# Halved blocks, output buffers and the last product of an attention-plus-gated-product kernel

## The chip, the core and the metric

The kernel runs on one NeuronCore of a Trainium2 chip. The metric is the device time of one execution in microseconds. Seven names recur: PE is TensorE's matmuls and PEld its weight loads, DVE is VectorE, ACT is ScalarE, POOL is GpSimd, SP is SyncE, and PSUM banks are where matmuls leave their sums (512 float32 columns on 128 partitions each).

## What is computed

The reference, cut to its core. There are 8 batches, 12 heads, 448 tokens of 64 numbers per head; the second part works on 3584 tokens of 768 numbers with 2048 hidden ones.

```python
scores = scale * np.matmul(q, k.transpose(0, 1, 3, 2))
attn = softmax(scores)                      # over the keys
x = np.matmul(attn, v)                      # heads side by side: (3584, 768)
h = x @ w_in                                # (3584, 2048)
g = h * (1.0 / (1.0 + np.exp(-h)))          # the gate
out = g @ w_out                             # (3584, 768), float32
```

## The kernel before

**Order.** Nothing is written in program order by hand. A planner (class `Order`, L111, with the loop at L1880) holds a queue of operations with durations and due times, and decides which engine does what next; the instructions are then emitted in that order (L1937). Each engine executes its own instructions strictly in sequence, with semaphores between the engines. A change of a few conditions in the planner can therefore move instructions far away from the edit.

**Attention.** A unit is a batch and a group of four heads (24 units, L987). For each unit, TensorE multiplies keys and queries in tiles of 32 rows (`score`, L436), ACT takes the exponential (`expo`, L479), TensorE forms sums and products with the values in strips of 32 columns (`attend_alone`, `attend_own`, `attend_shared`), and DVE transposes, inverts and scales (`inverse`, L611, and `norm`, L642) into the tile `xT`, which has the tokens in its columns. Batch 0's third group of heads is done in two halves of 224 tokens (`PIECES`, L253; the extra units 24 and 25), so that work on the first half can begin early.

**First product.** `ffn1` (L684) multiplies 128 hidden columns of `w_in` (a block; there are 16) with the tokens of a batch: six matmuls, one for each 128 rows of `w_in`. In batch 0 it does this for each half of the tokens by itself (224 columns), and puts two blocks side by side into one bank, so that one tanh on ACT and one gate on DVE (`tanh` L702, `gate` L734) cover 448 columns. Later batches use all 448 tokens and one block per bank. `queue_ffn1` (L1147) queues this; `blocks(b)` (L699) says how many blocks share a bank. Four banks, taken in turn, serve the attention sums, the first products and the outputs until the scores are finished. While attention is in progress, full-width products may be issued as four strips of 32 columns (`times`, L670).

**Batches 4 to 7** use a form of Strassen's seven products for the first matrix product (`pair_product`, L833), with operands combined by DVE into buffers that attention has finished with (`HOME`, L825; tags `E0` to `E9` are the exponentials' buffers).

**Second product.** Batch 0's first tiles are multiplied plainly (`plain`, L926). All other output tiles go in pairs, "quads" 1 to 13, again by seven products m = 1 to 7 of 8 steps each (`product`, L910; 384 columns a step). Products 1, 6, 7 and 4 add up in one bank, 5 and 3 in a second, 2 in a third. What a bank holds is read between: ACT copies it to a buffer `ost` (`take_copy`, L976), DVE adds a bank to that buffer (`take_sum`, L981). The order of products is 1, 5, 6, 2, 7, 3, 4. `store` (L956) then writes a finished buffer of 128 rows to memory in pieces of 32, 64 or 128 rows, from SP or in turn from SP and ACT. There are four `ost` buffers; quads 11 and 13 (`FAR`) use `xT` buffers instead.

**The end.** The last instructions are product 4 of quad 13 (8 matmuls of 384 columns), ACT's copy of its bank, and two stores of 64 rows, one from SP and one from ACT.

Of the kernel before, what the change touches and what calls it, by code (L numbers as in the profile page):

```python
# [9 lines left out]
FP16 = mybir.dt.float16  # L10
# [204 lines left out]
def kernel(  # L215
# [25 lines left out]
    OH = DM // 2  # L241
    NRK, NRQ = 2, 4
    PACE = 2.6
    NPL = 4
    EAGER = 1
    HALVES = 0
# [2 lines left out]
    SHY = 0.5  # L249
    AWAIT = 1.0  # L250
    FAR = (NT * B // 4 - 3, NT * B // 4 - 1)
    TWB, SXB = 40, 4
    PIECES = ((0, 7), (7, TPP))  # L253
    BURSTS = (
# [427 lines left out]
    h_t, th_t, o_t = {}, {}, {}  # L682

    def ffn1(b, f, t0, t1, strips, c0, c1):  # L684
        i = f % blocks(b)
        if i == 0 and c0 == 0:
            h_t[(b, f, t0)] = psum_bank(f"h_{b}_{f}_{t0}")
        h = h_t[(b, f - i, t0)]
        for cc in range(c0, c1):
            times(  # L690
                h[:, (t1 - t0) * i : (t1 - t0) * (i + 1)],
                w_in_t[:, cc, 128 * f : 128 * (f + 1)],
                x3(b, cc)[:, cc % 3, t0:t1],
                cc == 0,
                cc == NDC - 1,
                strips,
            )

    def blocks(b):  # L699
        return 2 if b == 0 else 1  # L700

    def tanh(b, f, t0, t1):  # L702
        n = (t1 - t0) * blocks(b)
        th = sb.tile([128, n], FP16, name=f"th_{b}_{f}_{t0}", tag="th", bufs=3)
        nc.scalar.activation(out=th, in_=h_t[(b, f, t0)][:, 0:n], func=AF.Tanh)  # L705
        th_t[(b, f, t0)] = th
# [27 lines left out]
    def gate(b, f, t0, t1):  # L734
        r = b % 2
        cut = 6 * 128 - S if b == 1 else S
        for lo, hi, dst, at in ((0, cut, G, S * r), (cut, S, X, -cut)):
            lo, hi = max(lo, t0), min(hi, t1)
            if b == 0 and lo < hi:
                nc.vector.scalar_tensor_tensor(  # L740
                    out=G[:, f : f + 2, t0:t1],
                    in0=th_t[(b, f, t0)].rearrange("p (f t) -> p f t", f=2),
                    scalar=1.0,
                    in1=h_t[(b, f, t0)][:, 0 : 2 * (t1 - t0)].rearrange("p (f t) -> p f t", f=2),
                    op0=ALU.add,
                    op1=ALU.mult,
                )
            elif lo < hi:
                nc.vector.scalar_tensor_tensor(  # L749
                    out=dst[:, f, at + lo : at + hi],  # L750
                    in0=th_t[(b, f, t0)][:, lo - t0 : hi - t0],
                    scalar=1.0,
                    in1=h_t[(b, f, t0)][:, lo - t0 : hi - t0],
                    op0=ALU.add,
                    op1=ALU.mult,
                )
# [150 lines left out]

    BANK = {1: 1, 6: 1, 7: 1, 4: 1, 2: 2, 5: 5, 3: 5}

    def product(qd, m, f0, f1, strips):  # L910
        w = {1: rows(2 * qd, 0), 2: rows(2 * qd, 1), 4: rows(2 * qd + 1, 1), 7: rows(2 * qd + 1, 0)}
        w = w[m] if m in w else S_t[(qd, m)]
        if BANK[m] == m and f0 == 0:
            pr_t[(qd, m)] = psum_bank(f"p_{qd}_{m}")
        for f in range(f0, f1):
            times(
                pr_t[(qd, BANK[m])][:, 0:OH],
                w[:, f, :],
                W_[m][:, f, :],
                f == 0 and BANK[m] == m,  # L920
                f == HF - 1,
                strips,
            )
# [19 lines left out]
    def bank(qd, m):  # L943
        return pr_t[(qd, m)][:, 0:OH]

    def ost(qd, i, j):
        name = f"ost_{qd}_{i}{j}"
        if qd in FAR:
            t = sb.tile([128, 3, S], FP16, name=name, tag="xT", bufs=NX3)
            t = t.rearrange("p c t -> p (c t)")[:, 0 : 2 * OH].bitcast(FP32)  # L950
        else:
            t = sb.tile([128, OH], FP32, name=name, tag="ost", bufs=NOST)
        ost_t[(qd, i, j)] = t
        return t

    def store(qd, i, j):  # L956
        u, t = divmod(2 * qd + i, NT)
        w, turn = 0, 0
        while w < 4:
            r, col = divmod(128 * t + 32 * w, S)  # L960
            b = 2 * u + r
            dst = out[b * S : (b + 1) * S, OH * j : OH * (j + 1)]
            if b == B - 1:
                n = 4 if w == 0 and qd < LAST else 2
                dst = dst[col : col + 32 * n]
            else:
                n = 1
                dst = dst.rearrange("(i g) m -> g i m", g=TPP)[col // 32]
            eng = nc.scalar if turn % 2 and 4 * qd + 8 >= NT * B else nc.sync
            eng.dma_start(out=dst, in_=ost_t[(qd, i, j)][32 * w : 32 * (w + n), :])  # L970
            w, turn = w + n, turn + 1

# [3 lines left out]
    def take_copy(qd, m):  # L976
        nc.scalar.copy(out=ost(qd, *OUT[m]), in_=bank(qd, BANK[m]))  # L977
        if m == 4:
            store(qd, *OUT[m])

    def take_sum(qd, m):  # L981
        t = ost_t[(qd, *SUM[m])]
# [137 lines left out]
    x_left = {}  # L1120
    ffn1_left = {b: 0 for b in range(B)}
    sg_ring, ost_ring = Ring(NSG), Ring(NOST)
    far_ring = Ring(NX3)
    STORE = 3.0
    pr_op, sg_op, w_op, plain_op = {}, {}, {1: [], 2: [], 3: []}, {}
    inv_op = []
# [11 lines left out]
    def gates_at(t, f):  # L1138
        if t % NT == NT - 1 and t // NT in KEPT:
            return [keep_op.get((t // NT, f // HF))]  # L1140
        made = []
        for b in {(128 * t + c) // S for c in (0, 127)}:
            x = g_op.get((b, f), [])
            made += x if len(x) >= (len(PIECES) if b == 0 else 1) else [None]
        return made

    def queue_ffn1(b, g0, g1):  # L1147
        t0, t1, parts = 32 * g0, 32 * g1, []
        begun = {}
        for f in range(NFF) if b == 0 else [x for f in range(HF if b < PB else FILL) for x in (f, f + HF)]:  # L1150

          half = 6 if b else NDC
          for c0 in range(0, NDC, half):

            def run(f=f, c0=c0):
# [2 lines left out]
                op = Op("PE", half * mm(t1 - t0), lambda: ffn1(b, f, t0, t1, strips, c0, c1), tail=PE_OUT)  # L1158
                if warm["on"]:
                    warm["on"] = False  # L1160
                n = blocks(b)
                if f % n == 0 and c0 == 0:
                    take_bank(f"h_{b}_{f}_{t0}")
                od.on_pe(op, "cols" if strips else "full", half * (4 if strips else 1))
# [24 lines left out]
            def deps(f=f, c0=c0):  # L1189
                if c0:  # L1190
                    return [] if begun.get(f) == c0 else [None]
                if f % blocks(b) and f - 1 not in parts:
                    return [None]
                made = [(x_op[(b, cc, g0)], cc * mm(t1 - t0)) for cc in range(NDC)] + ld_win[f]

                u, r = divmod(b, 2)
                for qd in range(NT * B // 4) if u else ():
                    if any(t // NT == u - 1 and (r or t % NT < 4) for t in (2 * qd, 2 * qd + 1)):
                        made += (
                            [plain_op.get(x) for x in ((0, 0), (0, 1), (1, 0), (1, 1))]  # L1200
                            if qd == 0
                            else [pr_op.get((qd, m)) for m in (1, 2, 3, 4, 7)]
                        )
                return made

            moe.append((deps, int(f % blocks(b) == 0 and c0 == 0), run, ()))
          ffn1_left[b] += 1

    pair_w, pair_x = {}, {}
# [80 lines left out]
    def queue_pair_f(pb, f):  # L1290
# [22 lines left out]
        def queue(m):  # L1313
# [6 lines left out]
            def run():  # L1320
# [7 lines left out]
                done[m] = op  # L1328
                if pb == PAIRS[0] and f == (3 if FILL < 4 else HF - 1) and m == 4:
                    last_pair.append(op)  # L1330
                if m == 1:
                    read("p", "ACT", lambda: pair_copy(pb, f, "p", "A"), [op], None, -3)
                elif m == 5:
# [59 lines left out]
    def queue_plain(t, j):  # L1393
# [6 lines left out]
        def queue(f0, f1):  # L1400
# [17 lines left out]
            def deps():  # L1418
# [2 lines left out]
                made = [ld_wout[i] for i in range(len(ld_wout)) if wout_rows[i] < f1]  # L1421
                for f in range(f0, f1):
                    x = g_op.get((0, f), ())
                    if len(x) < len(PIECES):
                        return [None]
                    made += x
                return made
# [56 lines left out]
    def queue_quad(qd):  # L1484
        quads.append((qd, [5, 6, 7, 3]))
        took = {}
        home = far_ring if qd in FAR else ost_ring

        def read(m, deps):
            def then(at):  # L1490
# [7 lines left out]
            bias = -2 if eng == "ACT" else -4  # L1498
            took[m] = od.add(Op(eng, busy, lambda: fn(qd, m), deps, bias, then=then))

        def queue(m, f0, f1):
            first = {6: (1,), 2: (1,), 7: (6, 5), 3: (5, 6) if qd == LAST else (5, 6, 7), 4: (7,)}.get(m, ())

            def run():
                strips = od.mode == "cols" and bool(qk_seq or av_seq)
                op = Op(
                    "PE", (f1 - f0) * mm(OH), lambda: product(qd, m, f0, f1, strips), tail=PE_OUT
                )
                if BANK[m] == m and f0 == 0:
                    take_bank(f"p_{qd}_{m}")  # L1510
                for ring, need in rings:
                    ring.take(need)
                if m in (5, 6, 3) and f1 == HF:
                    op.then = lambda at: sum_read(qd, m, at)
                od.on_pe(op, "cols" if strips else "full", (f1 - f0) * (4 if strips else 1))
                if f1 < HF:
                    begun[m] = f1
                    return
                pr_op[(qd, m)] = op
                read(m, [op] + [took[x] for x in {2: (1,), 7: (5,), 3: (6,)}.get(m, ())])  # L1520

            def deps():
                if f0:
                    return [] if begun.get(m) == f0 else [None]
                made = list(w_op.get(m, [None]))
                hard = {6: (1,), 7: (6,), 3: (5,), 4: (7,)}.get(m, ())
                made += [took.get(x) if x in hard else (took.get(x), 9.0) for x in first]
# [11 lines left out]


        begun = {}
        for m in (1, 5, 6, 2, 7, 3, 4):
            for f0 in range(0, HF, 1):
                queue(m, f0, f0 + 1)

    def after_x(n):

# [4 lines left out]
        else:  # L1552
            after_piece(b, g0, g1)

    def after_piece(b, g0, g1):
        x_left[(b, g0)] = x_left.get((b, g0), NG) - 1
        if x_left[(b, g0)]:
# [3 lines left out]
        if b >= PB:  # L1561
            return
        queue_ffn1(b, g0, g1)
        if g1 < TPP:
            return
        if b == 0:
# [402 lines left out]
```

## Time and profile before

| | us |
|---|---|
| median of 3 runs | 381.12 (380.66 to 381.26) |
| the profiled execution | 380.37 |
| its span, first to last instruction | 378.6 |
| TensorE busy in the span | 372.4 |
| DVE, ACT, POOL busy | 269.7, 255.5, 84.9 |
| granted TensorE clock | 1.0 |

The profile shows one execution. A group of instructions is given with its line, engine, operation and tile, how many there were, their busy time and the mean duration of one, which for pipelined matmuls is longer than the distance from one to the next. What an engine waited for is named by its releaser. The chain follows the end of the execution back, at each step to what released it, and can be listed in order of time. The order of a program's instructions on each engine is known without a run and holds no times.

### The profile page before, as it was taken

To read this page: it belongs to the slowest core of one execution; us is meant where nothing else is said; L and a number is where in the kernel's file an instruction comes from. 1 tells how busy PE (TensorE), PEld (TensorE's weight loads), DVE (VectorE), ACT (ScalarE), POOL (GpSimd) and SP (SyncE) were. 2 spreads that over 40 slices of the span, in tenths; PEclk is the share of its full clock that TensorE was granted. 3 is DMA by queue.
4 is the path that set the end of the run, shared out by engine and by line. 5 is a ranking of instruction groups with operands and counts; after the bars stand their busy time and mean duration, and the time that the engine had idled before them with its cause. 6 is when DMAs were issued, how large, how long until landed. Compare 5 with 4: busy or idle time off the path is not lost.

```text
span 378.6 us, 9949 instructions
## 1 busy us (share of the span) xinstructions
PE 372.4 (98%) x4024; PEld 191.5 (51%) x4024; DVE 269.7 (71%) x553; ACT 255.5 (67%) x400; POOL 84.9 (22%) x155
## 2 busy tenths in 40 slices
PE   7999999999999999999999999999999999999995
PEld 3367664444444444444444454545555555556663
DVE  3666859899995869995969998898475424446541
ACT  4988874897768787877788777658872238882221
POOL 6652438451007326006423200000000000000000
PEclk9999999999999999999999999999999999999999
DMA  7999999946139948148955421200002331002343
GB/s 120 191 208 210 206 204 186 190 53 98 17 92 124 184 49 124 26 94 116 170 86 73 54 53 34 68 18 0 3 1 59 94 74 26 0 2 59 84 110 83
DMA packets 35854, 34.47 MB, mean 91 GB/s; under 512 B 11872, under 2 KB 35040, under 8 KB 35808
## 3 DMA queue, kind: packets, MB, share of 16 engines
q0 software_dynamic: 25312, 22.82, 40.3%
q1 hardware_dynamic: 10080, 10.53, 10.6%
q8 instruction: 31, 0.51, 0.5%
q10 hardware_dynamic: 416, 0.49, 0.4%
q14 instruction: 15, 0.12, 0.1%
HBM read 45.61 MB, written 11.01 MB: 150 GB/s over the span
## 4 chain that ended last, share of the span: by engine, by line
PE 97%; DMA 1%; ACT 1%; DVE 0%; issue 0%; POOLq 0%
PE p L673 32%; PE h L673 21%; PE f L673 16%; PE s L438 12%; PE a L558 8%; PE o L673 3%; PE a L544 2%; PE a L591 2%; DMA rk<-in_k_dram 1%; ACT T L483 1%; PE z L1872 0%; PE z L673 0%; PE z L544 0%; DVE KT L387 0%; ACT ost L977 0%
## 5 line engine op out<-in xcount | busy, mean ns | idle before, releaser
L494 ACT ACTIVATE E<-s 128x896 f16<-128x896 f32 x164 | 142.0, 923 | 23.7 <-PE s L438 23.6
L673 PEld LDWEIGHTS <-w_in_t 128*128 128x128 f16 (+1 forms) x981 | 61.3, 97 | 45.2 <-issue 8.4
L673 PE MATMUL h<-xT,w_in_t 128*32 128x448 f16 (+2 forms) x834 | 84.0, 333 | 0.0
L344 POOL DMA_DIRECT2D V<-in_v_dram x88 | 48.4, 557 | 52.5 <-PE a L558 32.2
L673 PEld LDWEIGHTS <-G 128*128 128x128 f16 (+1 forms) x637 | 43.4, 97 | 32.4 <-issue 5.2
L977 ACT COPY ost<-p 128x384 f32<-128x384 f32 x52 | 24.9, 479 | 50.4 <-PE p L673 31.9
L705 ACT ACTIVATE th<-h 128x448 f16<-128x448 f32 x67 | 36.6, 546 | 22.8 <-PE h L673 19.1
L673 PE MATMUL p<-w_out_t,G 128*128 128x384 f16 (+1 forms) x343 | 51.9, 326 | 0.0
L438 PE MATMUL s<-rq,KT 32*128 32x448 f16 (+3 forms) x728 | 45.4, 347 | 1.3 <-DVE rq L402 1.0
L983 DVE TENSOR_TENSOR ost<-p,ost 128x384 f32<-128x384 f32 x39 | 21.6, 553 | 31.3 <-PE p L673 14.3
L673 PEld LDWEIGHTS <-S 128*128 128x128 f16 (+1 forms) x330 | 29.5, 98 | 23.5 <-issue 4.2
L673 PE MATMUL p<-D,S 128*128 128x384 f16 (+1 forms) x214 | 37.5, 326 | 0.0
L558 PE MATMUL a<-E,V 128*32 128x448 f16 (+1 forms) x640 | 32.9, 356 | 0.0
L749 DVE SCALAR_TENSOR_TENSOR G<-th,h 128x448 f16<-128x448 f16 (+1 forms) x52 | 28.8, 565 | 4.5 <-ACT th L705 3.9
L324 POOL DMA_DIRECT2D rq<-in_q_dram x25 | 13.8, 553 | 67.3 <-PE s L438 57.7
L661 DVE SCALAR_TENSOR_TENSOR xT<-a,rdn 128x448 f16<-128x448 f32 x46 | 27.0, 618 | 2.7 <-PE a L558 2.0
L438 PEld LDWEIGHTS <-KT 32*128 32x128 f16 (+1 forms) x824 | 12.5, 96 | 30.3 <-issue 28.1
L507 DVE TENSOR_TENSOR T<-T,E 128x1792 f16<-128x1792 f16 x20 | 21.7, 1086 | 3.9 <-ACT E L494 3.8
L876 DVE TENSOR_TENSOR p<-f,p 128x448 f32<-128x448 f32 x15 | 9.4, 624 | 20.4 <-PE f L673 13.5
L673 PE MATMUL f<-sx,tw 128*128 128x448 f16 x102 | 23.5, 352 | 0.0
L507 DVE TENSOR_TENSOR T<-E,E 128x1792 f16<-128x1792 f16 x20 | 21.6, 1082 | 2.5 <-ACT E L494 2.5
L558 PEld LDWEIGHTS <-V 128*32 128x32 f16 (+1 forms) x640 | 13.7, 95 | 18.0 <-issue 10.3
(95 smaller groups left out, 430.2 us busy)
## 6 DMA issues: line engine op xcount, KB each, us to landing
out_dram<-ost SPq DMA_DIRECT2D x194, 48.0 KB, 1.6
rk<-in_k_dram POOLq DMA_DIRECT2D x24, 224.0 KB, 5.0
rq<-in_q_dram POOLq DMA_DIRECT2D x23, 224.0 KB, 5.6
w_out_t<-in_moe_w_out_dram POOLq DMA_DIRECT2D x4, 768.0 KB, 12.5
V<-in_v_dram POOLq DMA_DIRECT2D x42, 64.0 KB, 4.1
V<-in_v_dram POOLq DMA_DIRECT2D x42, 48.0 KB, 4.3
w_in_t<-in_moe_w_in_dram POOLq DMA_DIRECT2D x6, 256.0 KB, 9.0
w_in_t<-in_moe_w_in_dram POOLq DMA_DIRECT2D x3, 512.0 KB, 12.3
```

The source lines that it names most:

```text
L324: nc.gpsimd.dma_start(out=rawq[n][:, cols], in_=group_of(q, b, hg)[:, cols])
L344: nc.gpsimd.dma_start(out=VT[b][32 * x : 32 * (x + 1), hs, at : at + count, :], in_=v[b, hs].rearrange("h (i g) d -> i h g d", g=TPP)[:, : ...
L438: nc.tensor.matmul(out=pS[p0 : p0 + 32 * (x1 - x0), h % 2, at : at + q1 - q0], lhsT=KT[(b, hg)][32 * h : 32 * (h + 1), key_rows(b, hg, c, ...
L494: nc.scalar.activation(out=E[(n, w)][:, 2 * y : 2 * y + 2, :], in_=pS_t[(n, w, y)][:, :, 0:S], func=AF.Exp, scale=attn_scale,)
L507: nc.vector.tensor_tensor(out=T[n], in0=T[n] if step else E[(n, 0)], in1=E[(n, step + 1)], op=ALU.add,)
L558: nc.tensor.matmul(out=a[32 * h : 32 * (h + 1), 0:S], lhsT=VT[b][k0:k1, HG * hg + h, place(b, hg, c), part - 1 :: 2], rhs=e[k0:k1, h], sta ...
L661: nc.vector.scalar_tensor_tensor(out=x3(b, cc)[:, cc % 3, 32 * g0 : 32 * g1], in0=acc[(n, part)][:, 0:nq], scalar=0.5, in1=rdn_t[n].rearra ...
L673: nc.tensor.matmul(out=out[i : i + cut], lhsT=w[:, i : i + cut], rhs=x, start=start, stop=stop, skip_group_check=True,)
L705: nc.scalar.activation(out=th, in_=h_t[(b, f, t0)][:, 0:n], func=AF.Tanh)
L749: nc.vector.scalar_tensor_tensor(out=dst[:, f, at + lo : at + hi], in0=th_t[(b, f, t0)][:, lo - t0 : hi - t0], scalar=1.0, in1=h_t[(b, f, ...
L977: nc.scalar.copy(out=ost(qd, *OUT[m]), in_=bank(qd, BANK[m]))
L983: nc.vector.tensor_tensor(out=t, in0=bank(qd, BANK[m]), in1=t, op=ALU.add)
```

## The change

Four things change, and the planner is told of each.

1. In batch 0 only blocks 0 to 3 are done in halves of the tokens (`BF0 = 4`). Blocks 4 to 15 wait for both halves, use 448 columns and one bank each, and have one tanh and one gate each. 
2. The outputs of quad 8 (`WIDE`) go to two of the ten `E` buffers, two outputs to each, in place of the four `ost` buffers. Those two held the first combined operands of batches 4 and 5, and count as free when the last block of that pair is done.
3. In the last quad product 2 comes last, and in two halves of 192 columns, each in a bank of its own. DVE adds each half to the buffer when it is done (`take_end`), SP stores the first half's 128 rows, SP and ACT store 64 rows each of the second.
4. The last quad's product 4, no longer last, is stored as one piece of 128 rows from ACT.

```diff
+    BF0 = 4
+    WIDE = NT * B // 4 - 6
...
-    def blocks(b):
-        return 2 if b == 0 else 1
+    def blocks(b, f):
+        return 2 if b == 0 and f < BF0 else 1
...
-    def product(qd, m, f0, f1, strips):
+    half_t = {}
+
+    def product(qd, m, f0, f1, strips, c0=0, c1=OH):
...
         if BANK[m] == m and f0 == 0:
-            pr_t[(qd, m)] = psum_bank(f"p_{qd}_{m}")
+            pr_t[(qd, m)] = psum_bank(f"p_{qd}_{m}" + "r" * (c0 > 0))
+        if c1 - c0 < OH:
+            half_t[c0] = pr_t[(qd, m)]
         for f in range(f0, f1):
             times(
-                pr_t[(qd, BANK[m])][:, 0:OH],
+                pr_t[(qd, BANK[m])][:, 0 : c1 - c0],
                 w[:, f, :],
-                W_[m][:, f, :],
+                W_[m][:, f, c0:c1],
...
+        elif qd == WIDE:
+            at, x = int(i != j), j
+            if at not in wide_t:
+                wide_t[at] = sb.tile(
+                    [128, HG, S], FP16, name=f"wide_{at}",
+                    tag=f"E{e_slot[f'sx_{PAIRS[0]}_{at + 1}']}", bufs=1,
+                )
+            t = wide_t[at].rearrange("p h s -> p (h s)").bitcast(FP32)
+            t = t[:, S * x : S * x + OH]
...
-                n = 4 if w == 0 and qd < LAST else 2
+                n = 4 if w == 0 and (qd < LAST or (i, j) == OUT[4]) else 2
...
+            if qd == LAST and (i, j) == OUT[4]:
+                eng = nc.scalar
...
+    def take_end(p, c0, c1):
+        t = ost_t[(LAST, 0, 0)][:, c0:c1]
+        nc.vector.tensor_tensor(out=t, in0=p, in1=t, op=ALU.add)
+        row = out.shape[0] - 256
+        for lo, eng in ((0, nc.sync), (64, nc.scalar)) if c0 else ((0, nc.sync),):
+            hi = lo + 64 if c0 else 128
+            eng.dma_start(out=out[row + lo : row + hi, c0:c1], in_=t[lo:hi])
...
-        for f in range(NFF) if b == 0 else [x for f in range(HF if b < PB else FILL) for x in (f, f + HF)]:
+        for f in range(BF0 * (g1 - g0 == TPP), NFF if g1 - g0 == TPP else BF0) if b == 0 else [x for f in range(HF if b < PB else FILL) for x in (f, f + HF)]:
...
-                made = [(x_op[(b, cc, g0)], cc * mm(t1 - t0)) for cc in range(NDC)] + ld_win[f]
+                made = [
+                    (x_op[(b, cc, g)], cc * mm(t1 - t0))
+                    for cc in range(NDC)
+                    for g in ((0, PIECES[1][0]) if b == 0 and g1 - g0 == TPP else (g0,))
+                ] + ld_win[f]
...
+                    for _ in range(4):
+                        wide_ring.give(op.done)
...
-        home = far_ring if qd in FAR else ost_ring
+        home = far_ring if qd in FAR else wide_ring if qd == WIDE else ost_ring
...
-        for m in (1, 5, 6, 2, 7, 3, 4):
+        for m in (1, 5, 6, 2, 7, 3, 4) if qd < LAST else (1, 5, 6, 7, 3, 4):
             for f0 in range(0, HF, 1):
                 queue(m, f0, f0 + 1)
+        if qd == LAST:
+            for c in range(2):
+                for f0 in range(0, HF, 1):
+                    queue(2, f0, f0 + 1, OH // 2 * c, OH // 2 * (c + 1))
...
+        if b == 0 and not pieces_left[b]:
+            queue_ffn1(b, 0, TPP)
```

More of the change, by code (lines that the diff above doesn't have):

```diff
@@ L684, in ffn1 @@
     def ffn1(b, f, t0, t1, strips, c0, c1):
-        i = f % blocks(b)
+        i = f % blocks(b, f)
         if i == 0 and c0 == 0:
@@ L697, in ffn1 @@
             )
-    def blocks(b):
-        return 2 if b == 0 else 1
+    def blocks(b, f):
+        return 2 if b == 0 and f < BF0 else 1
     def tanh(b, f, t0, t1):
-        n = (t1 - t0) * blocks(b)
+        n = (t1 - t0) * blocks(b, f)
         th = sb.tile([128, n], FP16, name=f"th_{b}_{f}_{t0}", tag="th", bufs=3)
@@ L738, in gate @@
             lo, hi = max(lo, t0), min(hi, t1)
-            if b == 0 and lo < hi:
+            if blocks(b, f) == 2 and lo < hi:
                 nc.vector.scalar_tensor_tensor(
@@ L944, in bank @@
         return pr_t[(qd, m)][:, 0:OH]
+    wide_t = {}
     def ost(qd, i, j):
@@ L1122 @@
     sg_ring, ost_ring = Ring(NSG), Ring(NOST)
-    far_ring = Ring(NX3)
+    far_ring, wide_ring = Ring(NX3), Ring(0)
     STORE = 3.0
@@ L1143, in gates_at @@
             x = g_op.get((b, f), [])
-            made += x if len(x) >= (len(PIECES) if b == 0 else 1) else [None]
+            made += x if len(x) >= blocks(b, f) else [None]
         return made
@@ L1160, in run @@
                     warm["on"] = False
-                n = blocks(b)
+                n = blocks(b, f)
                 if f % n == 0 and c0 == 0:
@@ L1191, in deps @@
                     return [] if begun.get(f) == c0 else [None]
-                if f % blocks(b) and f - 1 not in parts:
+                if f % blocks(b, f) and f - 1 not in parts:
                     return [None]
-                made = [(x_op[(b, cc, g0)], cc * mm(t1 - t0)) for cc in range(NDC)] + ld_win[f]
+                made = [
[3 more added lines that the diff above has]
+                ] + ld_win[f]
                 u, r = divmod(b, 2)
@@ L1204, in deps @@
                 return made
-            moe.append((deps, int(f % blocks(b) == 0 and c0 == 0), run, ()))
+            moe.append((deps, int(f % blocks(b, f) == 0 and c0 == 0), run, ()))
           ffn1_left[b] += 1
@@ L1423, in deps @@
                     x = g_op.get((0, f), ())
-                    if len(x) < len(PIECES):
+                    if len(x) < blocks(0, f):
                         return [None]
@@ L1499, in read, with queue @@
             took[m] = od.add(Op(eng, busy, lambda: fn(qd, m), deps, bias, then=then))
-        def queue(m, f0, f1):
+        def queue(m, f0, f1, c0=0, c1=OH):
             first = {6: (1,), 2: (1,), 7: (6, 5), 3: (5, 6) if qd == LAST else (5, 6, 7), 4: (7,)}.get(m, ())
@@ L1506, in run @@
                 op = Op(
-                    "PE", (f1 - f0) * mm(OH), lambda: product(qd, m, f0, f1, strips), tail=PE_OUT
+                    "PE",
+                    (f1 - f0) * mm(c1 - c0),
+                    lambda: product(qd, m, f0, f1, strips, c0, c1),
+                    tail=PE_OUT,
                 )
                 if BANK[m] == m and f0 == 0:
-                    take_bank(f"p_{qd}_{m}")
+                    take_bank(f"p_{qd}_{m}" + "r" * (c0 > 0))
                 for ring, need in rings:
@@ L1515, in run @@
                 od.on_pe(op, "cols" if strips else "full", (f1 - f0) * (4 if strips else 1))
+                if f1 < HF or c1 < OH:
+                    begun[m] = (HF if c0 else 0) + f1
                 if f1 < HF:
-                    begun[m] = f1
+                    return
+                if c1 - c0 < OH:
+                    fn = lambda: take_end(half_t[c0][:, 0 : c1 - c0], c0, c1)
+                    od.add(Op("DVE", 0.33, fn, [op, took[1]], -4))
                     return
@@ L1522, in deps @@
             def deps():
-                if f0:
-                    return [] if begun.get(m) == f0 else [None]
+                if f0 or c0:
+                    return [] if begun.get(m) == (HF if c0 else 0) + f0 else [None]
                 made = list(w_op.get(m, [None]))
@@ L1553, in after_x @@
             after_piece(b, g0, g1)
+    pieces_left = {}
     def after_piece(b, g0, g1):
@@ L1563, in after_piece @@
         queue_ffn1(b, g0, g1)
+        pieces_left[b] = pieces_left.get(b, len(PIECES) if b == 0 else 1) - 1
+        if b == 0 and not pieces_left[b]:
+            queue_ffn1(b, 0, TPP)
         if g1 < TPP:
```

## The prediction

> **What bounds the kernel now.** I read the page first, then TensorE's waits, its instructions by form, the chain in order of time, and the timeline of the last 12 us. The page:
>
> ```profile
> PE 372.4 (98%) x4024; PEld 191.5 (51%) x4024; DVE 269.7 (71%) x553; ACT 255.5 (67%) x400; POOL 84.9 (22%) x155
> ...
> PE   7999999999999999999999999999999999999995
> ...
> PE 97%; DMA 1%; ACT 1%; DVE 0%; issue 0%; POOLq 0%
> ```
>
> TensorE works from the second slice to the last and makes 97% of the chain. ACT and DVE have a quarter to a third of the span free, so what is saved there is worth nothing unless TensorE waits for it. It hardly does; its waits, in full:
>
> ```profile
> PE s L438 <- DVE rq L402: 1.0, 1, 1.0
> PE z L1872 <- DVE zeros L285: 1.0, 1, 1.0
> ```
>
> Both lie before 6.2 us. From the starts of the matmul records I find only two more hold-ups after 24 us: 0.2 us between 24.2 and 25.5 us, and 0.26 us at 249.8 us, both in stretches where the two programs have the same order. So the time is the sum of TensorE's matmuls and of its changes of shape, plus the stores after the last matmul. Pieces of the chain in order of time (start, us, what) price both:
>
> ```profile
> 29.57 2.98 PE h L673 x30
> 33.06 2.41 PE h L673 x24
> ...
> 76.61 0.51 PE s L438 x8
> 77.11 2.38 PE h L673 x12
> ...
> 83.59 2.27 PE h L673 x48
> ...
> 339.59 35.12 PE p L673 x216
> ```
>
> Less the 0.106 us of the change that follows, the 30 matmuls of 224 columns take 95.8 ns each and the 24 take 96.0; I use 95.9. Twelve 448-column ones take 2.27 us when nothing changes (the 48 are the same work in strips), so 189.2 ns each, and 2.38 when scores follow: leaving full width costs 0.11. A 384-column one takes 35.12/216 = 162.6 ns.
>
> **The change, step by step.** The order of instructions of both programs (it holds no time) is identical up to the second group of attention sums of batch 0, about 27.7 us in.
>
> 1. *Blocks 4 to 15 of batch 0 at full width.* 144 matmuls of 224 columns become 72 of 448: 144 x 95.9 = 13.81 us against 72 x 189.2 = 13.62, **-0.19 us**. Tanh and gate instructions stay 16 each on 448 columns (8 pairs in 2 halves, now 2 pairs in 2 halves and 12 blocks), so ACT and DVE neither gain nor lose.
>
> 2. *Changes of shape.* TensorE changes between full 128x128 weights, 32-row scores, and 32-column strips on 128 or 64 rows. I counted these changes in both orders: 200 before, 198 after. By the median excess of each kind in the trace: full to scores 1 less (106 ns), scores to full 1 less (85), strips to scores 2 more (106 each), scores to 64-row strips 1 more (83), 64-row to 128-row strips 1 more (124), and one less each of 128-row to 64-row strips (97), 64-row strips to full (126), full to 64-row strips (104) and 64-row strips to scores (126). The sum is **-0.22 us**. Twelve plain-product steps move into strips; a strip group of 384 columns takes 162.6 ns as the full one, so that costs nothing.
>
> 3. *The wait that is added.* Block 4 now needs the second half of batch 0's tokens earlier than any work did. In the timeline (start, us, engine and line, tile, idle before):
>
> ```profile
> 27.74 1.32 PE L673 MATMUL h<-xT,w_in_t 128*128 128x224 f16 x12
> 27.78 0.41 DVE L631 STREAM_TRANSPOSE rdn<-inv 128x224 f32<-128x224 f32 x1
> 28.30 0.62 DVE L650 SCALAR_TENSOR_TENSOR xT<-a,rdn 128x448 f16<-128x448 f32 x1
> ```
>
> Now six narrow matmuls go from 27.74 to 28.31, then block 4 begins. Its first four matmuls read rows that have long been there; the fifth, at 28.31 + 4 x 0.189 = 29.07, needs the DVE result of 28.92. At the same wait of the first half TensorE went on 0.06 us after DVE, so it is ready at 28.98: 0.09 us to spare, cost 0. Behind it in TensorE's order stands everything; late by x is late by x. The matmuls that used to cover it are gone; it could cost up to 0.2 us.
>
> 4. *Quad 8's outputs in buffers of their own.* The page's group waits show ACT and DVE idle 11.8 and 3.2 us for output stores to free a buffer. TensorE never stopped there: it filled in with products of other tiles, and p to f to p costs no change of shape. The new buffers are free when the first pair's last block is done, which precedes quad 8. Worth **0**; SP issues the same stores.
>
> 5. *The last quad in a new order.* Product 2 moves to the end in two column halves: 16 matmuls of 192 columns for 8 of 384. No row has 192; between the narrowest rows, 57 ns (128 columns, the zeros at 7.0 us) and 95.9 (224), a line gives 82.8. 16 x 82.8 - 8 x 162.6 = **+0.02 us**. Three of its steps now stand between products whose bank must be read first. Product 4 follows product 7 by 4 x 162.6 + 3 x 82.8 = 0.90 us; DVE begins 0.27 us after a product, takes 0.56 (timeline below), and 0.06 to release: 0.89. It just fits; at worst some 0.1 us.
>
> A rule speaks against this step. The loads of weights lie beside the matmuls here: the page's LDWEIGHTS rows have 97 ns of duration each, yet 224-column matmuls with a load each follow every 95.9 ns, and two 128-column zeros follow after 57. *The Trainium skill, "TensorE: Matmul & The Clock Gate", section "LDWEIGHTS (loading the stationary operand)", prices a load at columns / 1.2 ns, an estimate of 107 ns for 128 columns, independent of the matmul. By it 16 halves would take 1.71 us, 0.39 more than my 1.32. The 95.9 and 57 ns of this trace disagree with it as a pace.*
>
> 6. *The tail.* Before:
>
> ```profile
> 373.23 1.46 PE L673 MATMUL p<-D,G 128*128 128x384 f16 x8
> 373.50 0.56 DVE L983 TENSOR_TENSOR ost<-p,ost 128x384 f32<-128x384 f32 x1 [0.74 <-PE p L673]
> 374.73 0.48 ACT L977 COPY ost<-p 128x384 f32<-128x384 f32 x1 [4.72 <-PE p L673]
> 375.24 0.50 ACTq L970 DMA_DIRECT2D out_dram<-ost  x1
> ```
>
> Call TensorE's end T (373.23 + 8 x 0.1626 = 374.53). ACT begins at T+0.20, SP and ACT issue 64 rows each at T+0.71; ACT's half lands last, 2.39 us later at T+3.10, and 0.96 us of closing follow. After: DVE begins at T+0.27 and adds 192 columns in 0.36 (0.558 for 384, 0.624 for 448 elsewhere: 1.03 ns a column), so the issue is at T+0.66, 0.05 earlier. The rows are half as long. ACT's 64 packets run 0.46 us of that landing at 66 ns each; 4-byte packets take 9 ns, so on a line 768 bytes take 37 ns: about 0.11 less. Ahead of the pair two 128-row stores now go out, product 4's from ACT at T-0.11 and the first half's from SP at T. Bounds: as fast as the 48 KB stores of the page (1.6 us to landing) the pair lands at T+2.26, -0.84; held up by a whole 128-row store (0.67 us of packets in this trace) it lands at T+3.73, +0.63. I take the row that it is nearest to, the 64-row pair: **-0.16 us**.
>
> **Sum.** -0.19 - 0.22 + 0 + 0 + 0.02 - 0.16 = -0.55 us. The profiled execution took 380.37 us (span 378.6 and 1.77 around it), so 379.82; it lies 0.75 under the median of 381.12, from which the same step gives **380.6 us**, -0.14%.
>
> **Rivals.**
> A. *The smaller stores land as the 48 KB ones do*: -0.41 + 0.02 - 0.84 = -1.23, 379.9 us. For it: the bytes are those. Against: the landing goes with rows and queue more than bytes (ACT's packets start 0.44 us after SP's in each such pair).
> B. *The final pair queues behind the two 128-row stores*: -0.39 + 0.63 = +0.24, 381.4 us. For it: in the trace SP's and ACT's stores start one after the other, not together. Against: those two are issued 0.7 us earlier, more than the 0.44 lag.
> C. *Slower: the scores fall behind.* In the new order the scores of units 6 to 8 stand up to 2.0 us later (unit 7 at 72.6 for 70.6 us, by adding up the rows), and by unit 12 must be back 0.4 us ahead. ACT has to do what it does from 82 to 123 us, by the busy time in stretches 30.65 us in 41, in some 39. If it can't, TensorE waits for them, up to 2.0 us: -0.55 + 2.0 = +1.45, 382.6 us. It decides only above 39 us of ACT work; 30.65 is 79%, and ACT idles 5.4 us there for scores.
> D. *Weight loads pace the 192-column matmuls* at their 97 ns: 16 x (97 - 82.8) = +0.23, so -0.32, 380.8 us. (The rule above would give 380.96.) Against: 57 and 95.9.
>
> **Chances.** What a measurement of this kernel can tell from no change is about 0.2%, 0.76 us. Forecast (380.2 to 380.9) 0.55, A 0.20, B 0.11, C 0.08, D 0.06. Faster by more than 0.2%: A and a fifth of the forecast, 0.32. Slower: C and a little of B, 0.10. Within: 0.58. The range reaches from A to B, 379.9 to 381.4; C is left out.
>
> **What would show it.** Right: TensorE's last matmul about 0.4 us earlier (near 374.1 us), no wait at block 4 near 29 us, no longer gap than 0.1 us anywhere behind, 192-column matmuls 82 to 83 ns apart, the last store issued 0.66 us after them and landed by 3.0. Wrong: gaps before the fifth matmul of block 4 or before product 4, scores waiting for ACT between 60 and 100 us, or a landing more than 2.6 us after the last issue. Times of the same binary spread 0.6 us here, as much as the whole effect.

## The result and the profile after

The changed kernel takes 379.80 us (median of 9 runs, 379.21 to 380.46); the kernel before, run beside it, 380.66 (9 runs, 380.21 to 381.26). The ratio is 0.9976, 95% interval 0.9967 to 0.9986: 0.9 us, or 0.24%, faster. The forecast was 380.6 us with a range from 379.9; the time is 0.1 us below that range.

The profiled execution took 379.57 us (380.37 before). From its page:

```profile
span 377.8 us, 9884 instructions
...
PE 371.8 (98%) x4002; PEld 185.3 (49%) x4002; DVE 270.1 (71%) x554; ACT 255.4 (68%) x400; POOL 85.0 (22%) x155
...
PE 96%; ACT 1%; DMA 1%; DVE 0%; issue 0%; POOLq 0%
```

TensorE has 22 matmul records less, is busy 0.6 us less, and still makes the chain. Its waits, in full (releaser, total us, times, longest):

```profile
PE s L440 <- DVE rq L404: 1.1, 1, 1.1
PE z L1922 <- DVE zeros L287: 1.0, 1, 1.0
PE s L440 <- ACT E L496: 0.2, 1, 0.2
```

The first two are those of before. The third is at 11 us, ahead of the first place where the two programs differ (27.7 us); the kernel before has 0.03 us there. So the change adds no wait to this list: none at block 4 near 29 us, none for scores between 60 and 100 us, none before product 4 of the last quad. The end, in the timeline (start, us, engine and line, tile, idle before):

```profile
373.29 0.33 PE L675 MATMUL p<-w_out_t,G 128*128 128x192 f16 x2
373.46 0.82 PE L675 MATMUL p_2r<-w_out_t,G 128*128 128x192 f16 x8
373.49 0.48 ACT L996 COPY ost<-p 128x384 f32<-128x384 f32 x1 [3.92 <-PE p L675]
373.66 0.36 DVE L1002 TENSOR_TENSOR ost<-p,ost 128x192 f32<-128x192 f32 x1 [1.08 <-PE p L675]
...
374.32 0.36 DVE L1002 TENSOR_TENSOR ost<-p_2r,ost 128x192 f32<-128x192 f32 x1 [0.30 <-PE p_2r L675]
374.71 0.50 ACTq L1006 DMA_DIRECT2D out_dram<-ost  x1
```

Where the last ACT store lands is in the issues of each kernel from 374.6 us on (KB, us from issue to landing), first the kernel before, then the changed one:

```profile
out_dram<-ost ACTq DMA_DIRECT2D x1, 96.0 KB, 2.4
```

```profile
out_dram<-ost ACTq DMA_DIRECT2D x1, 48.0 KB, 2.1
```

The records of the last matmuls start 81 to 84 ns apart, so TensorE's end T is 374.12 us, 0.41 earlier than before. DVE's second addition begins at T+0.20, SP and ACT issue at T+0.58 and T+0.59, SP sees the last landing at T+2.72, and the span ends at T+3.68; before it was T+0.71, T+3.10 and T+4.07. So 0.41 us came from TensorE and 0.39 from the tail: 0.80 us, which is the difference of the two profiled times (380.37 and 379.57).

### The profile page after: what moved, and what is told of

Same layout as the page of the kernel before. It is cut to its first block, busy times and chain, and to the rows that moved or that the text cites. A ratio compares the mean times of both kernels' runs of the same rounds, so it can differ in the third digit from the quotient of the medians.

```text
span 377.8 us, 9884 instructions
## 1 busy us (share of the span) xinstructions
PE 371.8 (98%) x4002; PEld 185.3 (49%) x4002; DVE 270.1 (71%) x554; ACT 255.4 (68%) x400; POOL 85.0 (22%) x155
## 4 chain that ended last, share of the span: by engine, by line
PE 96%; ACT 1%; DMA 1%; DVE 0%; issue 0%; POOLq 0%
PE p L675 32%; PE h L675 21%; PE f L675 16%; PE s L440 12%; PE a L560 8%; PE o L675 3%; PE a L546 2%; PE a L593 2%; DMA rk<-in_k_dram 1%; ACT T L485 1%; PE z L675 0%; PE z L1922 0%; PE z L546 0%; ACT E L496 0%; PE p_2r L675 0%
## 5 line engine op out<-in xcount | busy, mean ns | idle before, releaser
L675 PE MATMUL h<-xT,w_in_t 128*32 128x448 f16 (+2 forms) x762 | 83.7, 348 | 0.0
L675 PEld LDWEIGHTS <-w_in_t 128*128 128x128 f16 (+1 forms) x909 | 54.5, 97 | 50.2 <-issue 8.4
L675 PEld LDWEIGHTS <-G 128*128 128x128 f16 (+1 forms) x696 | 44.2, 97 | 32.0 <-issue 5.0
L675 PE MATMUL p<-w_out_t,G 128*128 128x384 f16 (+2 forms) x334 | 51.9, 324 | 0.0
L996 ACT COPY ost<-p 128x384 f32<-128x384 f32 x48 | 23.0, 479 | 42.1 <-PE p L675 33.2
L675 PEld LDWEIGHTS <-S 128*128 128x128 f16 (+1 forms) x321 | 29.6, 98 | 23.1 <-issue 3.4
L751 DVE SCALAR_TENSOR_TENSOR G<-th,h 128x448 f16<-128x448 f16 (+1 forms) x64 | 35.9, 573 | 6.3 <-ACT th L707 5.8
L1010 DVE TENSOR_TENSOR ost<-p,ost 128x384 f32<-128x384 f32 x35 | 19.4, 553 | 28.8 <-PE p L675 13.4
L675 PE MATMUL p<-D,S 128*128 128x384 f16 (+1 forms) x217 | 37.5, 327 | 0.0
L675 PE MATMUL f<-sx,tw 128*128 128x448 f16 x102 | 23.4, 352 | 0.0
```

The costliest lines, as they stand in the source:

```text
L675: nc.tensor.matmul(out=out[i : i + cut], lhsT=w[:, i : i + cut], rhs=x, start=start, stop=stop, skip_group_check=True,)
L751: nc.vector.scalar_tensor_tensor(out=dst[:, f, at + lo : at + hi], in0=th_t[(b, f, t0)][:, lo - t0 : hi - t0], scalar=1.0, in1=h_t[(b, f, ...
L1010: nc.vector.tensor_tensor(out=t, in0=bank(qd, BANK[m]), in1=t, op=ALU.add)
```

## The experiments

Medians below stand beside the kernel before's of the same batch of runs, and all the profiles come from one execution each.

**The parts alone.** Each kernel has one part of the change, and the fourth is the whole change with one thing more.

```diff
# e1_blocks: BF0 = 4 alone        e2_wide: WIDE alone        e3_end: the last quad alone
# e5_one_store: the whole change, and in take_end
-        for lo, eng in ((0, nc.sync), (64, nc.scalar)) if c0 else ((0, nc.sync),):
-            hi = lo + 64 if c0 else 128
+        for lo, eng in ((0, nc.sync),):
+            hi = 128
```

> Only the blocks of batch 0 change (blocks 4 to 15 at full width); quad 8's buffers and the last quad are as before. Theory: TensorE saves 0.41 us (0.19 from merged matmuls, 0.22 from two fewer changes of shape), the tail stays 3.1 us from TensorE's end to the last landing; time -0.41 us, ratio 0.9989, last matmul starting near 374.0 us. Rival, that blocks carry the whole 0.8 us: ratio 0.998 with the last matmul near 373.6 us.

> Only quad 8's outputs get their own buffers. Theory: TensorE never waited for those buffers, so the order of its fill-ins changes and its time does not: ratio 1.000, last matmul near 374.4 us. Rival, that the idle time of ACT and DVE at these buffers (11.8 and 3.2 us) was worth something: ratio 0.999 or less and fewer TensorE gaps between 280 and 320 us.

> Only the last quad changes (product 2 last, in halves; product 4 as one store). Theory: TensorE +0.03 us, and the last store lands 2.7 us after TensorE's end where it was 3.1; time -0.36 us, ratio 0.9991. Rival, the forecast's own size: the tail gives 0.16, ratio 0.9996; in the profile the landing 2.9 us after TensorE's end.

> The changed kernel, with the second half of the last product stored as one piece of 128 rows from SP in place of 64 rows each from SP and ACT. Theory, that a second store has to wait for the first one's descriptors (ACT's packets start after SP's in each pair) and 128 rows alone start 0.87 us after issue: landing some 2.2 us after TensorE's end in place of 2.7, time 0.5 us under the changed kernel, ratio to before 0.9965. Rival, that the delay goes by rows, 128 rows in one or two pieces alike: landing at 2.7 us, ratio 0.9977.

| kernel | median, us | before, us | ratio (95%) |
|---|---|---|---|
| e1_blocks | 380.82 | 380.83 | 0.9996 (0.9987 to 1.0005) |
| e2_wide | 380.66 | 380.83 | 0.9998 (0.9989 to 1.0007) |
| e3_end | 380.15 | 380.83 | 0.9983 (0.9974 to 0.9992) |
| e5_one_store | 379.80 | 380.83 | 0.9966 (0.9953 to 0.9978) |

The end alone repeats the tail of the whole change to the hundredth (issue T+0.58, landing T+2.72, end T+3.68). One store of 128 rows in place of two of 64 lands at T+2.43 and ends at T+3.39, 0.29 us earlier; expected was a landing near T+2.2. Its median is the changed kernel's, 379.80 us, and the intervals of the two ratios overlap, so the gain stands in the profile alone. The blocks alone gave nothing that the times show, where 0.4 us was expected (the expected 0.9989 lies just inside the interval). Their chain around 290 us (start, us, what):

```profile
280.93 14.30 PE p L675 x88
295.23 0.02 ACTq L994
295.25 0.04 issue
295.29 0.49 ACT ost L994
295.78 0.04 issue
295.82 4.06 PE p L675 x24
```

In the kernel before the same stretch is one piece, 18.20 us of 112 matmuls. Here TensorE stands for 0.74 us between the 88th and the next, until ACT has copied a bank; the time from its first matmul on the first products to its end, 351.08 us, would be 350.34 without that, where the kernel before has 350.58. (Another 0.25 us of gap is near 56.4 us: TensorE waits there for the last piece of `w_out`, which landed at 56.57 us; in the changed kernel it landed at 56.05, just in time.) ACT's copy was late because one of the four `ost` buffers wasn't free: from 287.1 us on SP issues a store of 32 rows every 0.46 us, each issue taking 0.42, but the issue at 291.67 us took 1.84. At 291.6 us the trace has a packet of 16 KB on the instruction queue (q8). A trace has 31 of those (e10_before_split 32); from one to the next TensorE's records count some 252 instructions on average. In the kernel before they came at 286.9 and 308.2 us. A theory follows: such a packet holds up the stores that it meets, and in quad 8 the four buffers pass that on to TensorE. Buffers of their own for quad 8 would then be worth 0.7 us with the new blocks, and nothing without them.

**The change without quad 8's buffers, and the packet moved.**

```diff
# e7_no_wide: the whole change, but
-    WIDE = NT * B // 4 - 6
+    WIDE = -1
# e8_blocks_shift: e1_blocks, and in run_zeros, in the first call only
+        at = at[:2] + [(j, 1) for j in range(8, n)]
```

> The changed kernel, with quad 8's outputs back in the four ost buffers. Theory (a store that a 16-KB instruction packet holds up reaches TensorE through the four buffers): the packet comes near 292.4 us, among quad 8's stores, an issue of 1.2 us or more on SP follows, and TensorE waits for ACT's copy of product 6 of quad 8 near 295 us, 0.3 to 0.8 us; the time is 0.3 to 0.75 us above the changed kernel's, a ratio to the kernel before of 0.9984 to 0.9996 where the changed kernel had 0.9976. Rival (the buffers of quad 8 are worth nothing, as forecast; the blocks' version alone lost its 0.74 us by chance): no wait above 0.1 us near 295 us in the profile, ratio 0.9976.

> The blocks' version alone (four halved blocks, four ost buffers), and TensorE's first warm-up on zeros, before any data is there, cut into 41 matmuls instead of 12 over the same columns: 29 matmuls more, 58 instructions, everything else the same. Theory: the instruction packets come each 256 instructions, so this one moves 29 x 0.1626 = 4.7 us earlier, from 291.6 to about 286.9 us, where the kernel before had it, ahead of quad 8's train of stores; the issues on SP between 288 and 295 us then take 0.42 us each, and TensorE's wait of 0.74 us at 295.2 us is gone: last matmul 0.5 to 0.9 us earlier relative to the first matmul on the first products, ratio to the kernel before about 0.9989 for 0.9996. Rival (the order of the blocks makes the wait, wherever the packet falls): the wait stays at 295.2 us and the ratio at 0.9996. The start may shift by 0.2 us either way.

Without the buffers the wait is back, and in e8_blocks_shift, with its packet at 289.4 us after a start 2.7 us late, it is gone. The waits of e7_no_wide:

```profile
PE p L675 <- ACT ost L996: 0.6, 1, 0.6
```

(The list has 0.6 us; from matmul to matmul the gap is 0.74.) The median is 380.81 us beside 380.49, ratio 1.0009 (0.9998 to 1.0020), where the whole change had 0.9976; that is more than the 0.9984 to 0.9996 expected. From the first matmul on the first products to TensorE's end it took 351.09 us, where the changed kernel took 350.06: 0.74 us of the difference is this wait, and 0.29 a wait for `w_out` near 56 us as in e1_blocks. The profiled execution of e8_blocks_shift (382.83 us, one of its two longest; the median is 380.65) ran into something unwanted: its first products began 2.7 us later (one wait of 1.7 us before 16.7 us, and a granted clock of 0.79 and 0.64 in the six us behind it), and its times spread from 379.72 to 383.06, so its ratio of 1.0009 (0.9994 to 1.0025) says little. From the first matmul on the first products to TensorE's end it took 350.07 us, 1.01 less than e1_blocks: the 0.74 of the wait, and the 0.25 near 56 us.

A cleaner shift splits full-width matmuls in the middle of the kernel, in the version that has the wait, to take it away, and in the kernel before, to make it:

```diff
# e9_no_wide_split: e7_no_wide with n = 30;  e10_before_split: the kernel before with n = 98; in ffn1
+            step = t1 - t0
+            if b and not strips and left[0]:   # left = [n]
+                left[0] -= 1
+                step = 224
+            for k in range(0, t1 - t0, step):
-                x3(b, cc)[:, cc % 3, t0:t1],
+                x3(b, cc)[:, cc % 3, t0 + k : t0 + k + step],
```

Where a matmul is split, the second half starts its sum in a bank that the first half already uses, so the sums of those blocks are not the reference's; the number, the widths and the order of the matmuls are as described.

> The changed kernel with quad 8 in the four ost buffers again, and the first 30 full-width matmuls of batch 1's first products split into two of 224 columns each: 60 instructions more between 80 and 200 us, for 30 x (2 x 95.9 - 189.2) = 0.08 us. Theory: the 16-KB instruction packet that came at 291.9 us comes 30 x 0.1626 = 4.9 us earlier, near 287.1 us, at the head of quad 8's train of stores; the wait of 0.6 us on ACT at 295 us is gone, and the time is that of the changed kernel with its own buffers plus 0.08: a ratio of 0.9978 to the kernel before. Rival (the order of the products makes the wait, and the version with moved warm-ups lost it by its late start): the wait stays, ratio 1.0009.

> The kernel before, with the first 98 full-width matmuls of batches 1 to 3's first products split into two of 224 columns: 196 instructions more, for 98 x 2.6 ns = 0.25 us. Theory: the packets come every 256 instructions, so the one at 308.2 us now comes 98 x 0.1626 = 15.9 us earlier, near 292.3 us, in the middle of quad 8's stores, where the version with fewer halved blocks had it: SP has an issue of 1.2 us or more near 292 us, TensorE waits 0.3 to 0.8 us for ACT near 295 us, though nothing of the change is in this kernel, and the ratio is 1.0015 to 1.0027. Rival: no such wait, ratio 1.0007.

Both came as the theory had it. e9_no_wide_split: the packet came at 286.7 us, the wait is gone (its chain has `PE p L675 x112` in one piece of 18.20 us again), 379.93 us beside 380.60, ratio 0.9987 (0.9977 to 0.9996; the 0.9978 expected is at its edge), against 1.0009 with the wait. In its profiled execution TensorE also stood still for 0.38 us near 25.4 us, ahead of the first split matmul; the changed kernel has no such gap there. e10_before_split: 381.44 us, ratio 1.0023 (1.0011 to 1.0034), its packet at 291.9 us. Its chain shows every link:

```profile
291.29 0.42 SPq L976
291.71 0.04 issue
291.75 2.02 SPq L976
293.78 0.04 issue
293.82 1.63 DMA out_dram<-ost
295.45 0.02 issue
295.47 0.04 ACTq L983
295.51 0.04 issue
295.55 0.49 ACT ost L983
296.04 0.04 issue
296.08 4.06 PE p L673 x24
```

SP is held for 2.02 us in one issue, the store behind it lands late, ACT's copy waits for its buffer, and TensorE for the copy. The DMA view of that kernel from 291 to 294 us shows the packet and the slow stores (packets, MB, share; below, the issues with KB and median us to landing):

```profile
q8 instruction: 1, 0.02, 3.1%
...
out_dram<-ost SPq DMA_DIRECT2D x4, 48.0 KB, 3.3
```

The kernel before has no such packet in that window, seven stores, and 1.6 us to landing:

```profile
out_dram<-ost SPq DMA_DIRECT2D x7, 48.0 KB, 1.6
```

The same holds all through the kernels: in the fourteen traces 117 store issues on SP took over 1 us, 116 of them overlap one of these packets, and nine in ten of those end 0.32 to 0.38 us behind the packet's end.

The changed kernel has the packet too, at 292.4 us. SP's issue at 292.61 us takes 1.19 us, but the next outputs go to `wide`, whose buffers are free, and TensorE doesn't notice.

**What the halves are worth.**

```diff
# e4_last_whole: the whole change, product 2 last but in one piece
-            for c in range(2):
-                for f0 in range(0, HF, 1):
-                    queue(2, f0, f0 + 1, OH // 2 * c, OH // 2 * (c + 1))
+            for f0 in range(0, HF, 1):
+                queue(2, f0, f0 + 1)
# e11_two_thirds: e5_one_store, cut at 256 columns
-            for c in range(2):
+            for c0, c1 in ((0, 256), (256, OH)):
# e6_quarters: the whole change, each 192-column matmul as two of 96
```

> The changed kernel with product 2 still last, but whole: eight matmuls of 384 columns into one bank, one DVE addition of 384 columns, two stores of 64 whole rows. By the measured tails: DVE begins 0.20 us after TensorE's end and takes 0.56, the issue is at T+0.79, the landing of a pair of 1536-byte rows 2.39 later (as in the kernel before) at T+3.18, end T+4.14; TensorE ends as in the changed kernel. So 0.46 us above the changed kernel, ratio 0.9988. Rival (the order of the products and who finishes is what helps, the halving nothing): landing at T+2.7 as in the changed kernel, ratio 0.9976.

> The changed kernel with its last half output as one 128-row store from SP, and product 2 cut at 256 columns instead of 192. TensorE: 8 x (57 + 109) against 16 x 82.8 ns, the same. DVE's last addition takes 128 columns, 0.29 us for 0.36; it starts at T+0.20, when the first piece's addition (0.42 us from T-0.26) has just ended at T+0.17; the last issue is at T+0.53 for T+0.59, unless SP is still at the first piece's store (issue T+0.20, 0.35 us), which makes it T+0.56. 128 packets of 512 bytes for 768: 0.05 to 0.1 us less. End at T+3.25 to T+3.30 for T+3.39. Ratio 0.9963 for 0.9966, which the times can't tell apart; the profile can.

> The changed kernel with the 16 matmuls of 192 columns at the end issued as 32 of 96 columns, each with its weight load. By the line through the rows for 128, 192 and 224 columns (57, 82.8 and 95.9 ns) 96 columns take 43 ns, so 32 take 1.38 us against 1.32. If the loads set the pace below some width, 97 ns each (their recorded duration) gives 3.1 us, and 107 ns each (the Trainium skill, "TensorE: Matmul & The Clock Gate", section "LDWEIGHTS (loading the stationary operand)") 3.4 us.

e4_last_whole: DVE T+0.20 to T+0.76, issue T+0.79, landing T+3.21 (expected 3.18), end T+4.23; 380.55 us, ratio 1.0002 (0.9993 to 1.0011), above the 0.9988 expected. The profile accounts for 0.55 us of its distance to the changed kernel; what the times show beyond that is open. So the new order of the products alone brings nothing to the tail; it ends 0.16 us later than before's T+4.07 (0.08 of it is DVE's addition, longer than ACT's copy). The halves bring 0.55 us of the tail. e11_two_thirds: the last issue came at T+0.69 and not T+0.56, because SP's first store was issued only at T+0.24, for 0.35 us, and the next followed 0.10 behind it; still the end is at T+3.32, 0.07 before the even cut. 379.72 us, ratio 0.9977 (0.9967 to 0.9987): by the times it is not told from the changed kernel, and the 0.9963 expected lies outside.

e6_quarters (one run, 380.32 us; splitting loses a term of that product's sums as above): the 96-column matmuls start 42 to 43 ns apart, each with a weight load of 97 to 98 ns recorded. The line through the rows had 43. A load's duration is no pace here, down to less than half of it. The Trainium skill, "TensorE: Matmul & The Clock Gate", section "LDWEIGHTS (loading the stationary operand)", gives columns / 1.2 ns, an estimate of 107 ns for such a load; as a bound on the pace these runs contradict it. The same page, section "Wait — 56ns, not 53.3ns?", gives columns / 2.4 + 2.5 ns from matmul to matmul at full clock: estimates of 42.5 and 82.5 ns, which the traces agree with (42.5 in this one, 82.6 in the changed kernel's).

**A step further that failed.** With the same rows, eight halved blocks instead of four looked better still.

```diff
# full_bf8: e5_one_store, and
-    BF0 = 4
+    BF0 = 8
```

> The changed kernel with eight blocks of batch 0 in halves instead of four, and the last half output stored as one 128-row store from SP. By the rows: 64 matmuls of 224 columns become 32 of 448 against the kernel before (64 x 95.9 - 32 x 189.2 = 0.08 us less), and the order has 188 changes of shape for 200, in all 1.2 us less on TensorE; the tail as measured with one store, 0.68 us less. Sum -1.9 us, ratio 0.995, about 0.6 us below the version with one store and four halved blocks. Rival (the changes of shape are not priced right by their medians, or the scores come late): TensorE as with four blocks, -0.4 us, ratio 0.9966.

It took 401.77 us, ratio 1.0570 (1.0543 to 1.0598). The waits of TensorE name it, and so does the clock in 40 slices:

```profile
PE s L440 <- ACT E L496: 9.9, 19, 1.0
```

```profile
PEclk9999999999999999999999997759999999999999
```

From 100 to 125 us ACT worked 13.97 us, in the changed kernel 19.06; from 150 to 175, 13.50 for 18.95; from 200 to 225, 13.55 for 19.36. The planner's new order put products ahead of scores: by 225 us TensorE had started 664 matmuls of scores, in the changed kernel 768, and 1278 of products for 1244. So ACT got its work late, and at the end of the attention no products were left to cover the exponentials: from 240.4 to 250.4 us TensorE had scores alone, and in all it waited 19 times for ACT. Then its clock fell. Windows of 5 us (PE busy, granted clock, DMA share, GB/s):

```profile
235.00:240.00 5.00, 4.24 (x80) 1.00 0.94 157
240.00:245.00 5.00, 2.30 (x32) 1.00 0.14 18
245.00:250.00 5.00, 3.05 (x30) 0.58 0.57 74
250.00:255.00 5.00, 4.75 (x56) 0.50 0.01 3
```

After 5 us at 46% the granted clock is half: the clock's record has 0.5 for 10.2 us from 245.8 us on, and again for 10.2 us from 262.9. The Trainium skill has this rule on the same page, section "What's actually happening": after an idle window of about 3.4 us the clock is halved. This trace agrees with the half, 0.50, but not with the idle window: the longest wait of TensorE in the stretch ahead of 245.8 us was 1.0 us. The count of matmuls and shape changes, which priced this kernel at -1.2 us, was no use at all once TensorE waited.

## Why the prediction was wrong in size

The step that failed is step 6, the tail: forecast at -0.16 us, measured at -0.39. The starting time was wrong besides. TensorE's part was right, and none of the rivals came true. That the time lies beside rival A's 379.9 us is chance: the last store did not land as A has it.

**Right: TensorE's part** (steps 1, 2 and 5). The forecast sum was -0.39 us and the last matmul ends 0.41 us earlier. Two things in it aren't the change's and nearly cancel: the first matmul on the first products came 0.11 us later, and a hold-up near 25 us was 0.14 shorter (0.19 before, 0.05 after). Without them 0.38 us is left. How it divides between steps 1 and 2 wasn't measured. The 192-column pace was 82.6 ns for 82.8.

**Right: the wait at block 4** (step 3) and the fit of product 4 behind product 7 (step 5): no gap in either place. Rivals B and D didn't happen, C not with four blocks; with eight blocks it is what happened, later in the kernel than thought.

**Wrong in size: the tail** (step 6), forecast -0.16, measured -0.39 us. The terms: the addition begins at T+0.20, not T+0.27, because the 0.27 was read from an addition that has two results to wait for, and DVE's record of the first wait stands 0.065 us ahead of it; the new addition waits for TensorE alone. And from the last issue to the landing it took 2.13 us, where 2.28 was forecast (2.39 less 0.11): ACT's first packet came 1.39 us after the issue for 1.57, the packets took 46 ns for 66, where the line had 37. A third of the way to rival A, not more.

**Wrong as a reason: quad 8's buffers are worth 0** (step 4). "TensorE never stopped there" was true of the trace of before, and the page's idle times of ACT and DVE were no loss. But that trace had the instruction packet at 286.9 us. The new blocks take 60 instructions from TensorE ahead of that, the packet moves 4.7 us, into the stores, and without the buffers 0.6 to 0.8 us of wait would be lost (0.74 to 0.93 from matmul to matmul; e1_blocks, e7_no_wide, and e10_before_split, which moves the packet alone). The sum came out right here, since the change brings the buffers along; as a price of step 4 alone, zero holds only for the old place of the packet (e2_wide: 0.9998).

**Wrong: the anchor**, the time that the step is taken from. The forecast took -0.55 us from 381.12, the median of three runs. In four batches with 9 to 29 runs the kernel before has medians of 380.49 to 380.83. The forecast step from 380.66 would have been 380.11; of the 0.3 us still missing, 0.23 is the tail. From the profiled execution the prediction had 379.82 us, and the profiled execution after took 379.57. The tail and the anchor put it past the 0.2% at which "no difference" was called likeliest.

**Open.** By its sum e1_blocks has 0.4 us less and 0.74 us of wait more on TensorE, so it should be 0.3 us slower than before (1.0009), and its interval ends at 1.0005. Its two stalls stand in one profiled execution; how much its other runs lose isn't shown. Nor is it shown why a packet holds up a store (whether it takes a DMA engine's turn or SP's own), only that the two coincide, move together, and that SP's issue ends when the packet has ended.

## What to carry to other kernels

A ring of buffers that shows no wait in one profile has a slack, and it should be read off (here SP's stores 0.46 us apart and four buffers): a DMA that the program doesn't contain can use it up, and any edit that changes the number of instructions moves that DMA. Price the tail by its own records from the last matmul on: which wait really starts the last operation, its issue, its first packet, its landing. And a sum of matmul times holds only as long as another engine's work, spread over the whole kernel, keeps its place; check where that engine stands in each stretch before trusting the count.

## What was not expected of the hardware

- 16-KB instruction packets delay stores: a 32-row store's issue on SP, usually 0.42 us, took 1.19, 1.84 and 2.02 us beside one. They come with TensorE's instructions, some 252 apart: 60 or 196 more of those moved them (e9_no_wide_split, e10_before_split). The issue that took 1.84 us did so in two different programs (e1_blocks, e7_no_wide).
- The granted clock fell to 0.50 after 5 us with TensorE busy at 46% and waits of at most 1.0 us (full_bf8).
- One store of 128 rows of 768 bytes from SP landed 0.29 us earlier than two of 64 rows from SP and ACT issued at the same time (T+2.43 for T+2.72).
- A DVE addition with two producers has a record of its own for the first wait, 0.065 us ahead of it, and began 0.27 us after TensorE's end; one that waits for TensorE alone began after 0.20.
